# Block attention that feeds two dense layers: the attention step taken for two pairs of heads at a time

## Chip, cores and metric

The kernel runs on one core of a Trainium2 chip. The metric is the device time of one execution in microseconds (us); lower is better.

## What is computed

q, k and v have shape (2, 8, 768, 64): 2 batches, 8 heads, 768 tokens, 64 channels. A query sees its neighbours closer than 16 tokens and, beside them, one summary column for each of the 24 blocks of 32 tokens: the maximum of the block's keys and the mean of its values. The result, 1536 tokens by 512 channels, goes through two pairs of dense layers.

```python
k_sum = k.reshape(B, H, nb, block, D).max(axis=3)
v_sum = v.reshape(B, H, nb, block, D).mean(axis=3)
scores = concat([where(|i - j| < 16, q k^T / 8, -1e9), q k_sum^T / 8 + log(32)])
a = exp(scores - max);  a = a / (sum(a) + 1e-9)
x = (a @ concat([v, v_sum])).transpose(0, 2, 1, 3).reshape(1536, 512)
h = x @ moe_w_in;   x = (h * clip(h + 3, 0, 6) / 6) @ moe_w_out      # w_in 512x2048, w_out 2048x512
h = x @ moe2_w_in;  out = (h * cos(h)) @ moe2_w_out
```

The dense weights arrive with 8 bytes an element, read by the kernel as pairs of 32-bit words.

## The kernel before

**Attention.** The 8 heads make 4 pairs; a pair fills 128 partitions (two heads of 64 channels). The work is cut into 24 units `(b, h, p)`: batch, third of the sequence (256 tokens), pair. One unit is one call of `att`:

- `score`: 8 products, each 64 channels by 64 queries against 120 columns (96 tokens around the queries and 24 summaries). In 32-bit floats each product is two matmul instructions, so 16. They use TensorE in tiles of 64x64 and write two banks of PSUM (`c_s`), one for each head of the pair.
- four times VectorE adds the mask and takes the maximum (L529), and ScalarE takes the exponential and its sum (L537).
- GpSimd, VectorE and either of them: sum plus 1e-9, its reciprocal, the multiplication (L546, L551, L555).
- `trans`: four transposes on the whole array into the one bank of `c_t` (L564), and a copy to `pt`.
- `pv`: 8 products (16 instructions) with tiles of 128 rows by 64 columns (L573), into the one bank of `c_o`; then `xh`, a copy rounded to the type `F32R`, and `xl`, what the rounding left (256 columns each).

For each batch and pair, `load_k` and `load_v` bring keys and values (576 KB each), `k_prep` takes the maxima (L497), and `vsum_pe` takes the block means with two TensorE products in tiles of 32 columns (L477: 24 instructions; L482: 2), two small copies and `fill`, which writes the means into all 12 windows of `vw`. `load_q` brings 128 KB for each unit into one of three buffers `z`.

**Dense layers.** Every product is made as three passes, high by high, high by low and low by high part (L667 to L669 for the first product of a layer pair, L743 for the second). A chunk of 128 of the 2048 inner columns has two halves of weights, each split into its parts by ScalarE, VectorE and GpSimd (L618, L622, L627, then L403 or L405, and L410). Blocks are 512 tokens, except that the very first block is two of 256 tokens. A first product needs `x` of all four pairs for its tokens. `post` makes the nonlinearity and the two parts of `g`.

**Order.** `Plan` holds every operation with its cost in us on the engines that may do it, a priority, and the buffers it takes. `order()` runs a list schedule over these costs on the host, and the instructions are issued in the order that it finds; each engine and the SP queue, which issues nearly all transfers, then work in that fixed order. `refine()` repeats this five times with priorities that come from deadlines. The numbers in `T` set the first priorities: `A0` and `AS` when unit after unit starts, `lk`, `lq`, `lv` the loads, `kp`, `vpe`, `fill` the preparation, `g0`, `gi`, `wc`, `wl` the dense layers; `nz`, `nraw`, `n2` and the like are counts of buffers. Up to `busy` us, small idle matmuls (L434, on the identity) fill gaps of TensorE in the plan. The cost of a TensorE operation is a constant, whatever stood ahead of it (`score` 0.58, `trans` 0.44, `pv` 0.62).

Buffers that only attention uses are given back when its last operation is issued (`turn`), and more buffers for the dense layers (`w`, `g`, `n`, `r`) take their place.

Of the kernel before, what the change touches and what calls it, by code (L numbers as in the profile page):

```python
# [18 lines left out]
P = 128  # L19
# [43 lines left out]
def consts():  # L63
# [53 lines left out]
class Op:  # L117
    __slots__ = ("engs", "fn", "prio", "port", "seq", "wait", "after", "ready", "takes", "uses", "start", "eng", "took")


class Plan:
# [10 lines left out]
    def op(self, engs, fn, prio, r=(), w=(), take=(), port=0.0):  # L132
        o = Op()
        o.engs, o.fn, o.prio, o.port, o.seq = engs, fn, prio, port, len(self.ops)
# [87 lines left out]

    def refine(self):
        best = None
        for n in range(T["n"]):
            if n:
                self.reset()
            try:
                order = self.order()
            except AssertionError:  # L230
                break
            end, late = self.deadlines(order)
            if best is None or end < best[0] - 1e-9:
                best = (end, [o.prio for o in self.ops])
            for o in self.ops:
                if "PE" not in o.engs:
                    o.prio = late[id(o)]
        self.end = best[0]
        for o, p in zip(self.ops, best[1]):
            o.prio = p  # L240
        self.reset()

    def order(self):
# [6 lines left out]
        free["DMA"] = T["d0"]  # L250

# [11 lines left out]
        while events:  # L263
# [11 lines left out]
            for e in names:  # L275
# [79 lines left out]
def body(ctx: ExitStack, tc: tile.TileContext, q, k, v, w_in1, w_out1, w_in2, w_out2, ident_d, mask_d, avg_d, out):  # L355
# [34 lines left out]
    c_r = slots("r", 2, [P, TOK], later=T["n2"])  # L390
# [62 lines left out]
    def load_q(b, h, p, prio):  # L453
        z = Buf(c_z)
        dma(lambda: z.t, lambda: q[b, p][:, HT * P * h:HT * P * h + HT * P], 0.54, prio, w=[z], take=[z])
        return z
# [13 lines left out]
    def vsum_pe(vw, prio):  # L470
# [3 lines left out]
        def mm(e):  # L474
            for s in range(NS):
                a, g = 2 * (NS - 1 - s), s % 4 * QD
                nc.tensor.matmul(out=bank.t[g:g + QD, 0:P], lhsT=avg[0:CW, a:a + QD], rhs=vw.t[0:CW, s, :],  # L477
                                 start=(s < 4), stop=(s >= NS - 4), tile_position=(0, g))
# [3 lines left out]
        op({"PE": 0.25}, lambda e: nc.tensor.matmul(out=bank.t[CW:P, P:2 * P], lhsT=avg[:, AW:AW + QD], rhs=y.t,  # L482
                                                    start=True, stop=True, tile_position=(0, CW)),
           prio, r=["avg", y], w=[bank])
        op({"ACT": 0.2, "DVE": 0.2}, lambda e: copy(e, x.t[CW:CE, :], bank.t[CW:CE, P:2 * P]), prio, r=[bank],
           w=[(x, 0), (x, 1)])
        return x

    def fill(x, vw, prio):
        op({"POOL": 1.5, "ACT": 1.55},  # L490
           lambda e: copy(e, vw.t[CW:CE, :, :], x.t[CW:CE, :].rearrange("p (u f) -> p u f", u=1).to_broadcast([NB, NS, P])),
           prio, r=[(x, 0), (x, 1)], w=[(vw, CW)], take=[vw])
# [12 lines left out]
    def att(b, h, p, kw, z, vw, prio, banks):  # L505
        sp = [Buf(banks) for _ in range(2)]
        e_, sm, pt, tp, res = Buf(c_e), Buf(c_sm), Buf(c_pt), Buf(c_t), Buf(c_o)
        N4 = 2 * HT
        subs = [(i, u, o) for i in range(HT) for u in range(2) for o in range(2)]

        def score(e):
            for i, u, o in subs:
                f = slice(D * o, D * o + D)
                a = i * P + u * SUB
                nc.tensor.matmul(  # L515
                    out=sp[o].t[u * SUB:u * SUB + SUB, i * CE:i * CE + CE], lhsT=z.t[f, a:a + SUB],
                    rhs=kw.t[f, 2 * (HT * h + i) + u, :], start=True, stop=True,
                )

        op({"PE": 0.58}, score, prio,  # L520
           r=[z, (kw, "own"), (kw, "sum")], w=sp, take=[*sp, e_, sm])
        for i in range(HT):
            t = HT * h + i
            mk = mask[:, 0 if t == 0 else (2 if t == TB - 1 else 1), :]
            for o in range(2):
                x = 2 * i + o
                op(
                    {"DVE": 0.2},
                    lambda e, i=i, o=o, x=x, mk=mk: nc.vector.tensor_tensor_reduce(  # L529
                        out=e_.t[:, x, :], in0=sp[o].t[:, i * CE:i * CE + CE], in1=mk,  # L530
                        scale=-0.125, scalar=3.0e38, op0=ALU.add, op1=ALU.min, accum_out=sm.t[:, x:x + 1],
                    ),
                    prio, r=[sp[o], "masks"], w=[(e_, x), (sm, x)],
                )
                op(
                    {"ACT": 0.38},
                    lambda e, x=x: nc.scalar.activation(  # L537
                        out=e_.t[:, x, :], in_=e_.t[:, x, :], func=ACTF.Exp, scale=-1.0,
                        bias=sm.t[:, x:x + 1], accum_out=sm.t[:, N4 + x:N4 + x + 1],
                    ),  # L540
                    prio, r=[(sm, x)], w=[(e_, x), (sm, N4 + x)],
                )
        sums = [(sm, N4 + x) for x in range(N4)]
        op(
            {"POOL": 0.2},
            lambda e: nc.gpsimd.tensor_scalar(  # L546
                out=sm.t[:, N4:2 * N4], in0=sm.t[:, N4:2 * N4], scalar1=1.0, scalar2=1e-9, op0=ALU.mult, op1=ALU.add
            ),
            prio, w=sums,
        )  # L550
        op({"DVE": 0.09}, lambda e: nc.vector.reciprocal(out=sm.t[:, N4:2 * N4], in_=sm.t[:, N4:2 * N4]), prio,  # L551
           w=sums)
        op(
            {"POOL": 1.05, "DVE": 0.57},
            lambda e: eng[e].tensor_tensor(  # L555
                out=e_.t, in0=e_.t,
                in1=sm.t[:, N4:2 * N4].rearrange("p (x u) -> p x u", u=1).to_broadcast([P, N4, CE]), op=ALU.mult,
            ),
            prio, r=sums, w=[(e_, x) for x in range(N4)], port=0.5,
        )  # L560

        def trans(e):
            for x in range(N4):
                nc.tensor.transpose(out=tp.t[0:CE, x * P:(x + 1) * P], in_=e_.t[:, x, :], identity=ident)  # L564

        op({"PE": 0.44}, trans, prio, r=[(e_, x) for x in range(N4)], w=[tp], take=[tp, pt])
        op({"ACT": 0.49, "DVE": 0.6}, lambda e: copy(e, pt.t[0:CE, :], tp.t[0:CE, :]), prio, r=[tp], w=[pt])

        def pv(e):
            for i, u, o in subs:  # L570
                f = slice(D * o, D * o + D)
                a, c = (2 * i + o) * P + u * SUB, i * P + u * SUB
                nc.tensor.matmul(out=res.t[f, c:c + SUB], lhsT=vw.t[0:CE, 2 * (HT * h + i) + u, f],  # L573
                                 rhs=pt.t[0:CE, a:a + SUB], start=True, stop=True)
# [4 lines left out]
        hi, lo, r = xh[j][:, p, c], xl[j][:, p, c], range(i, i + HT)  # L579
        op({"ACT": 0.28, "DVE": 0.34}, lambda e: copy(e, hi, res.t[:, 0:HT * P]), prio, r=[res],  # L580
           w=[("xh", j, p, i) for i in r])
        op({"DVE": 0.33}, lambda e: sub(e, lo, res.t[:, 0:HT * P], hi), prio,
           r=[res, *(("xh", j, p, i) for i in r)], w=[("xl", j, p, i) for i in r])
# [4 lines left out]
    units = []  # L588
# [3 lines left out]
    for y, (b, h, p) in enumerate(units):  # L592
        pr = A0 + AS * HT * y
        if h == 0:
            kws[p], ks = load_k(b, p, pr + T["lk"])
        z = load_q(b, h, p, pr + T["lq"])
        if h == 0:
            vws[p] = load_v(b, p, pr + T["lv"])
# [225 lines left out]
```

## Time and profile before

| what | us |
|---|---|
| median of 3 runs | 610.3 (610.02 to 610.71) |
| the profiled execution, its own time | 610.45 |
| its span, first to last instruction | 608.7 |
| TensorE busy in the span | 602.1 (99%) |
| VectorE, GpSimd, ScalarE busy | 387.2, 347.0, 268.8 |

The span is 1.75 us shorter than the execution's own time. The granted TensorE clock is 1.00 of full speed (2.4 GHz) in every stretch of 10 us. A matmul's busy time in these views is longer than the step from its start to the next one's start, because matmuls overlap; where a time on TensorE is worked out below, it is taken from starts.

### The profile page before, as it was taken

How to read it: one execution, taken by the hardware profiler on the slowest of the kernel's cores; microseconds unless marked ns; L12 is line 12 of the kernel's file. 1: busy time of each engine (PE TensorE's matmuls, PEld its weight loads, DVE VectorE, ACT ScalarE, POOL GpSimd, SP SyncE). 2: the span in 40 equal slices, each digit the busy share in tenths (PEclk: the TensorE clock that was granted, in tenths of full speed). 3: DMA queues.
4: the chain of work that ended last, by engine and by line, in shares of the span. 5: the costliest groups of instructions: out<-in, count | busy, mean ns of one | idle time of the engine just before them, and what ended most of it. 6: DMA issues, size and time to landing. Idle time of an engine off the chain costs nothing.

```text
span 608.7 us, 9662 instructions
## 1 busy us (share of the span) xinstructions
PE 602.1 (99%) x3636; PEld 498.6 (82%) x3636; DVE 387.2 (64%) x724; ACT 268.8 (44%) x585; POOL 347.0 (57%) x366
## 2 busy tenths in 40 slices
PE   9999999999999999999999999999999999999997
PEld 8878877788888888888888888888888888888886
DVE  3599894443852258523993589857984897574562
ACT  2698886533421114301351547654752363343240
POOL 2588784555853438623688398656864577443340
PEclk9999999999999999999999999999999999999999
DMA  9978950042420004300440013301320020000112
GB/s 224 269 240 246 255 184 22 1 138 70 138 70 0 1 7 167 105 0 1 140 137 0 1 69 104 104 2 68 105 103 2 1 103 1 1 2 0 70 42 97
DMA packets 28334, 50.07 MB, mean 82 GB/s; under 512 B 14464, under 2 KB 17920, under 8 KB 28288
## 3 DMA queue, kind: packets, MB, share of 16 engines
q1 hardware_dynamic: 28144, 49.40, 26.4%
q8 instruction: 28, 0.46, 0.3%
q14 instruction: 18, 0.15, 0.1%
q10 hardware_dynamic: 144, 0.07, 0.0%
HBM read 46.31 MB, written 3.15 MB: 81 GB/s over the span
## 4 chain that ended last, share of the span: by engine, by line
PE 94%; DVE 2%; POOL 1%; ACT 1%; issue 1%; DVEq 0%; POOLq 0%; ACTq 0%
PE acc L743 25%; PE s L743 18%; PE h L667 8%; PE h L668 8%; PE h L669 8%; PE o L669 3%; PE t L669 3%; PE o L667 3%; PE t L667 3%; PE o L668 3%; PE t L668 3%; PE acc L434 2%; PE s L515 2%; PE o L573 2%; PE t L564 2%; PE h L477 1%
## 5 line engine op out<-in xcount | busy, mean ns | idle before, releaser
L405 POOL TENSOR_SCALAR g<-r 128x512 fp32r<-128x512 f32 (+1 forms) x81 | 61.9, 764 | 135.4 <-DVE r L718 40.8
L410 POOL TENSOR_TENSOR g<-r,g 128x512 fp32r<-128x512 f32 (+1 forms) x73 | 100.5, 1377 | 7.3 <-ACT g L403 2.8
L699 ACT ACTIVATE n<-h,bias 128x512 f32<-128x512 f32 (+1 forms) x60 | 39.3, 656 | 141.3 <-PE h L669 139.3
L743 PE MATMUL acc<-g,w 128*128 128x512 f32 (+1 forms) x432 | 96.0, 370 | 0.0
L667 PE MATMUL h<-xh,w 128*128 128x512 f32 (+1 forms) x240 | 92.5, 386 | 0.0
L668 PE MATMUL h<-xl,w 128*128 128x512 f32 (+1 forms) x240 | 90.0, 375 | 0.0
L669 PE MATMUL h<-xh,w 128*128 128x512 f32 (+1 forms) x240 | 90.0, 375 | 0.0
L743 PEld LDWEIGHTS acc<-g,w 128*128 128x128 f32 x432 | 75.3, 188 | 14.3 <-issue 0.8
L703 DVE SCALAR_TENSOR_TENSOR r<-n,h 128x512 f32<-128x512 f32 (+1 forms) x60 | 38.7, 646 | 56.8 <-ACT n L699 31.0
L743 PE MATMUL acc<-w,g 128*128 128x512 f32 x288 | 69.2, 389 | 0.0
L743 PE MATMUL s<-w,g 128*128 128x512 f32 x288 | 69.2, 389 | 0.0
L410 POOL TENSOR_TENSOR w<-cf,w 128x512 fp32r<-128x512 f32 x44 | 64.1, 1460 | 3.3 <-ACT w L403 1.6
L743 PEld LDWEIGHTS acc<-w,g 128*128 128x128 f32 x288 | 54.1, 188 | 11.2
L743 PEld LDWEIGHTS s<-w,g 128*128 128x128 f32 x288 | 54.0, 188 | 11.2
L627 DVE SCALAR_TENSOR_TENSOR cf<-cu,cf 128x512 uint32<-128x512 uint32 x64 | 60.0, 955 | 0.4
L618 ACT ACTIVATE cu<-raw 128x512 f32<-128x512 f32 x64 | 42.9, 670 | 38.5 <-DVE cf L627 23.7
L622 DVE TENSOR_SCALAR cf<-raw 128x512 uint32<-128x512 uint32 x64 | 47.3, 755 | 11.8 <-POOL w L410 11.6
L667 PEld LDWEIGHTS h<-xh,w 128*128 128x128 f32 x240 | 45.1, 188 | 9.9 <-issue 1.7
L711 POOL TENSOR_SCALAR n<-n 128x512 f32<-128x512 f32 x45 | 31.8, 707 | 37.3 <-ACT n L699 37.2
L669 PEld LDWEIGHTS h<-xh,w 128*128 128x128 f32 x240 | 45.1, 188 | 8.2
L668 PEld LDWEIGHTS h<-xl,w 128*128 128x128 f32 x240 | 45.1, 188 | 7.8
L405 POOL TENSOR_SCALAR w<-cf 128x512 fp32r<-128x512 f32 x41 | 31.4, 770 | 30.3 <-DVE cf L627 23.2
(95 smaller groups left out, 1054.7 us busy)
## 6 DMA issues: line engine op xcount, KB each, us to landing
raw<-in_w_in_dram SPq DMA_DIRECT2D x32, 512.0 KB, 4.1
raw<-in_w_out_dram SPq DMA_DIRECT2D x32, 512.0 KB, 3.7
kw<-in_k_dram SPq DMA_DIRECT2D x8, 576.0 KB, 6.0
vw<-in_v_dram SPq DMA_DIRECT2D x8, 576.0 KB, 9.3
z<-in_q_dram SPq DMA_DIRECT2D x24, 128.0 KB, 5.7
out_dram<-part SPq DMA_DIRECT2D x8, 256.0 KB, 2.0
out_dram<-kw SPq DMA_DIRECT2D x3, 256.0 KB, 2.0
out_dram<-kw SPq DMA_DIRECT2D x2, 128.0 KB, 1.7
```

The lines of the kernel that those rows point to most:

```text
L405: eng[e].tensor_scalar(out=out, in0=in_, scalar1=scale, scalar2=0.0, op0=ALU.mult, op1=ALU.add)
L410: eng[e].tensor_tensor(out=out, in0=in0, in1=in1.bitcast(F32), op=ALU.subtract)
L618: lambda e, raw=raw, u=u: nc.scalar.activation(out=u.t, in_=raw.t.bitcast(F32)[:, :, 1], func=ACTF.Prelu, scale=2.0 ** -112, alpha=2.0 ** 32),
L622: lambda e, raw=raw, f=f: eng[e].tensor_scalar(out=f.t.bitcast(U32), in0=raw.t[:, :, 0], scalar1=2.0 ** -29, scalar2=7.0, op0=ALU.mult, op ...
L627: lambda e, u=u, f=f: nc.vector.scalar_tensor_tensor(out=f.t.bitcast(U32), in0=u.t.bitcast(U32), scalar=3, in1=f.t.bitcast(U32), op0=ALU.l ...
L667: nc.tensor.matmul(out=o, lhsT=wh, rhs=hi, start=(kk == 0), stop=False)
L668: nc.tensor.matmul(out=o, lhsT=wh, rhs=lo, start=False, stop=False)
L669: nc.tensor.matmul(out=o, lhsT=wl, rhs=hi, start=False, stop=(kk == KT - 1))
L699: op({"ACT": t(fixed, 0.43)}, lambda e: nc.scalar.activation(out=out(), in_=in_(), func=func, **kw), pr, r=rd, w=wr, take=take)
L703: op({"DVE": t(0.09, 0.56)}, lambda e: nc.vector.scalar_tensor_tensor(out=out(), in0=a(), scalar=s, in1=b(), op0=o0, op1=o1), pr, r=rd, w= ...
L711: op({"POOL": t(0.16, 0.47), "DVE": t(0.07, 0.265)}, lambda e: eng[e].tensor_scalar(out=n(), in0=n(), scalar1=1.0, scalar2=-MAGIC, op0=ALU ...
L743: nc.tensor.matmul(out=o, lhsT=l, rhs=r, start=(c == 0 and z == 0), stop=(c == GS - 1 and z == 2))
```

## The change

Attention is taken for two pairs of heads at a time. The units become `(b, h, p, ny)`: the first two stay single, and then there are 11 of two pairs each. In such a unit `score` issues 16 products in one go (columns 0 to 479 of the same two banks), and `pv` 16 into one whole bank of `c_o`; `xh` and `xl` are made once for 512 columns. The mask, exponential, sums, multiplication, transposes and copies to `pt` stay as they were, pair by pair. `load_q` moves both pairs at once (256 KB). `vsum_pe` takes the values of two pairs: 48 instructions into one bank, one copy, one second product over 256 columns, one copy; `fill` stays one for each pair.

Buffers: `z` 3 of one pair become 2 of two, `vs` 2 become 1 of two, `e` 3 become 2 of two, `sm` 4 become 2 of two; `r` of the dense layers has 1 in place of 2 until `turn`.

The plan: every TensorE operation has a tiling `mode` (0 dense, 1 transpose, 2 score, 3 pv, 4 sums of v), and `change(a, b)` adds a price where it differs from the one before. The costs of the attention operations are set without it. All numbers in `T` are new.

```diff
 T = dict(
-    A0=6.982, AS=1.584, mask=-12.92, kp=-20.41, qp=-33.47, lk=-17.33, lq=-11.81, lv=-4.43, vs=33.64, vss=-16.92,
-    vsp=-29.27, wl=-1.64, wc=-25.07, g0=20.77, gi=7.33, pp=27.42, fill=-9.73, DVE=1.348, POOL=0.497, cold=5, d0=0.9,
-    warm=9, tail=1, lagq=1, nraw=3, ncf=2, n=5, w2=2, n2=3, g2=3, nz=3, busy=42, slack=0.2, vpe=-7.47, avg=-27.4,
+    A0=5.118, AS=1.568, mask=-8.22, kp=-14.19, qp=-15.92, lk=-15.36, lq=-11.42, lv=-4.09, vs=37.77, vss=27.87,
+    vsp=-18.03, wl=-15.78, wc=-15.19, g0=20.42, gi=5.51, pp=17.22, fill=-28.29, DVE=1.348, POOL=0.572, cold=5, d0=0.9,
+    warm=9, tail=1, lagq=3, nraw=3, ncf=2, n=5, w2=2, n2=3, g2=3, nz=2, nr=1, busy=42, slack=0.2, vpe=-45.26,
+    avg=-8.5,
 )
...
+    @staticmethod
+    def change(a, b):
+        if a == b:
+            return 0.0
+        return (0.165 if a > 1 else 0.0) + (0.19 if b > 1 else 0.1 if b else 0.0)
...
+                if e == "PE":
+                    cost += self.change(mode, o.mode)
+                    mode = o.mode
...
-    c_z = slots("z", T["nz"], [P, HT * P], pool=ap)
+    c_z = slots("z", T["nz"], [P, 2, HT * P], pool=ap)
...
-    c_vs = slots("vs", 2, [P, P], pool=ap)
-    c_y = slots("y", 1, [P, P], pool=ap)
+    c_vs = slots("vs", 1, [P, 2, P], pool=ap)
+    c_y = slots("y", 1, [P, 2, P], pool=ap)
...
-    c_e = slots("e", 3, [P, 2 * HT, CE], pool=ap)
-    c_sm = slots("sm", 4, [P, 4 * HT])
+    c_e = slots("e", 2, [P, 4 * HT, CE], pool=ap)
+    c_sm = slots("sm", 2, [P, 8 * HT])
...
-    c_r = slots("r", 2, [P, TOK], later=T["n2"])
+    c_r = slots("r", T["nr"], [P, TOK], later=T["n2"])
...
-        op({"PE": 0.85}, mm, prio, r=["avg", (vw, 0)], w=[bank], take=[bank, x, y])
-        op({"ACT": 0.2, "DVE": 0.2}, lambda e: copy(e, y.t, bank.t[:, 0:P]), prio, r=[bank], w=[y])
+            for i, vw in enumerate(vws):
...
+        op({"PE": 1.36}, mm, prio, r=["avg", *((vw, 0) for vw in vws)], w=[bank], take=[bank, x, y], mode=4)
+        op({"ACT": 0.3, "DVE": 0.34}, lambda e: copy(e, both(y.t), bank.t[:, 0:2 * P]), prio, r=[bank], w=[y])
...
+            for y in range(ny):
+                for i, u, o in subs:
...
-        op({"PE": 0.58}, score, prio,
+        op({"PE": 0.41 * ny}, score, prio,
+           r=[z, *((kw, x) for kw in kws for x in ("own", "sum"))], w=sp, take=[*sp, e_, sm], mode=2)
...
-        op({"PE": 0.44}, trans, prio, r=[(e_, x) for x in range(N4)], w=[tp], take=[tp, pt])
+            op({"PE": 0.425}, trans, prio, r=[(e_, x) for x in xs], w=[tps[y]], take=[tps[y], pts[y]], mode=1)
...
-        op({"PE": 0.62}, pv, prio, r=[pt, (vw, 0), (vw, CW)], w=[res], take=[res])
+        op({"PE": 0.44 * ny}, pv, prio, r=[*pts, *((vw, x) for vw in vws for x in (0, CW))], w=[res], take=[res], mode=3)
...
-    for p in range(NP + T["lagq"]):
-        units += [(0, 0, p)] * (p < NP) + [(0, 1, p - T["lagq"])] * (p >= T["lagq"])
-    units += [(b, h, p) for b in range(B) for h in range(NH) for p in range(NP) if b or h > 1]
+    units = [(0, 0, 0, 1), (0, 0, 1, 1), (0, 0, 2, 2)]
+    units += [(b, h, p, 2) for b in range(B) for h in range(NH) for p in range(0, NP, 2) if b or h]
```

## Rows read from the trace of the kernel before

**Rows 1.** Page, part 4: the chain that ended last, share by engine.
```profile
PE 94%; DVE 2%; POOL 1%; ACT 1%; issue 1%; DVEq 0%; POOLq 0%; ACTq 0%
```
**Rows 2.** Busy time by stretch: start and end, length, us (instructions) of each engine, clock, DMA.
```profile
0.00:26.00 26.00, 24.94 (x282) 22.83 (x282) 9.86 (x51) 10.10 (x39) 8.46 (x20) 1.00 1.00 250
26.00:53.00 27.00, 25.23 (x381) 20.96 (x379) 25.61 (x91) 24.05 (x81) 21.38 (x24) 1.00 0.78 243
53.00:90.00 37.00, 36.80 (x537) 30.48 (x535) 34.54 (x121) 32.46 (x116) 29.53 (x35) 1.00 0.81 217
90.00:118.00 28.00, 28.00 (x299) 21.33 (x297) 12.17 (x61) 18.09 (x63) 13.75 (x19) 1.00 0.09 30
118.00:605.18 487.18, 487.14 (x2150) 403.03 (x2148) 304.25 (x402) 184.04 (x291) 273.92 (x269) 1.00 0.17 57
```
**Rows 3.** Chain that ended last, stretches 26 to 54 us, then 53 to 118, by line.
```profile
by line: DVE cf L627 15.9%; issue 10.0%; DVE cf L622 8.3%; POOL w L405 8.0%; DVE w L410 6.3%; PE s L515 6.2%; ACT e L537 5.8%; DVE e L529 5.7%; POOL e L555 5.0%; POOL w L410 4.6%; DVE xl L410 3.9%; PE t L564 3.5%; PE h L477 2.8%; PE o L573 
...
by line: PE acc L743 22.9%; PE o L573 13.3%; PE t L564 11.4%; PE h L667 11.1%; PE s L515 10.5%; PE h L668 8.1%; PE h L669 8.0%; PE h L477 3.7%; POOL e L555 2.2%; POOL w L410 2.0%; ACT e L537 1.8%; PE h L482 1.0%; ACT pt L403 0.9%; ACT cu L6
```
**Rows 4.** Timeline of PE around one score; last two from windows inside it (start, us).
```profile
102.28 0.39 PE L669 MATMUL h<-xh,w 128*128 128x512 f32 x1
102.60 0.64 PE L515 MATMUL s<-kw,z 64*64 64x120 f32 x16
103.17 0.50 PE L667 MATMUL h<-xh,w 128*128 128x512 f32 x1
103.51 0.40 PE L668 MATMUL h<-xl,w 128*128 128x512 f32 x1
...
102.86 0.39 PE L515 MATMUL s<-kw,z 64*64 64x120 f32 x8
102.96 0.28 PE L515 MATMUL s<-kw,z 64*64 64x120 f32 x4
```
**Rows 5.** The same around one pv.
```profile
106.34 0.39 PE L669 MATMUL h<-xh,w 128*128 128x512 f32 x1
106.66 0.69 PE L573 MATMUL o<-pt,vw 120*64 120x64 f32 x16
107.27 0.50 PE L667 MATMUL h<-xh,w 128*128 128x512 f32 x1
107.61 0.40 PE L668 MATMUL h<-xl,w 128*128 128x512 f32 x1
...
106.94 0.40 PE L573 MATMUL o<-pt,vw 120*64 120x64 f32 x8
107.06 0.29 PE L573 MATMUL o<-pt,vw 120*64 120x64 f32 x4
```
**Rows 6.** Stretch 53 to 118 us, lines L515, L573, L477: PE (instructions), PEld, clock, DMA.
```profile
53.00:118.00 65.00, 8.34 (x208) 5.36 (x208) 1.00 0.50 137
53.00:118.00 65.00, 10.94 (x256) 8.79 (x256) 1.00 0.50 137
53.00:118.00 65.00, 3.45 (x96) 2.38 (x96) 1.00 0.50 137
```
**Rows 7.** Groups of instructions: evacuation of one pair, and copies of 512 columns.
```profile
L403 ACT ACTIVATE xh<-o 128x256 fp32r<-128x256 f32 x23 | 8.7, 378 | 3.5 <-PE o L573 3.4
L410 DVE TENSOR_TENSOR xl<-o,xh 128x256 fp32r<-128x256 f32 x24 | 10.0, 417 | 12.0 <-ACT xh L403 11.8
L403 ACT ACTIVATE part<-acc 128x512 f32<-128x512 f32 x8 | 4.7, 591 | 3.1 <-PE acc L743 3.1
L766 DVE TENSOR_TENSOR part<-part,acc 128x512 f32<-128x512 f32 x26 | 17.7, 682 | 19.3 <-PE acc L743 19.3
```
**Rows 8.** Timelines of PE and of the SP queue in the first 37 us.
```profile
19.03 4.90 PE L434 MATMUL acc<-ident 128*128 128x64 f32 x42
23.86 0.86 PE L477 MATMUL h<-vw,avg 96*32 96x128 f32 x24
35.14 0.39 PE L667 MATMUL h<-xh,w 128*128 128x256 f32 x1
36.21 0.86 PE L477 MATMUL h<-vw,avg 96*32 96x128 f32 x24
...
18.80 0.33 SPq L437 DMA_DIRECT2D raw<-in_w_in_dram  x1
26.91 0.33 SPq L437 DMA_DIRECT2D z<-in_q_dram  x1
27.29 0.44 SPq L437 DMA_DIRECT2D vw<-in_v_dram  x1
```

More of the change, by code (lines that the diff above doesn't have):

```diff
@@ L117 @@
 class Op:
-    __slots__ = ("engs", "fn", "prio", "port", "seq", "wait", "after", "ready", "takes", "uses", "start", "eng", "took")
+    __slots__ = ("engs", "fn", "prio", "port", "seq", "wait", "after", "ready", "takes", "uses", "start", "eng", "took", "mode")
 class Plan:
@@ L483, in vsum_pe, with fill @@
                                                     start=True, stop=True, tile_position=(0, CW)),
-           prio, r=["avg", y], w=[bank])
-        op({"ACT": 0.2, "DVE": 0.2}, lambda e: copy(e, x.t[CW:CE, :], bank.t[CW:CE, P:2 * P]), prio, r=[bank],
-           w=[(x, 0), (x, 1)])
+           prio, r=["avg", y], w=[bank], mode=4)
+        op({"ACT": 0.3, "DVE": 0.34}, lambda e: copy(e, both(x.t)[CW:CE, :], bank.t[CW:CE, 2 * P:4 * P]), prio, r=[bank],
+           w=[x])
         return x
-    def fill(x, vw, prio):
+    def fill(x, i, vw, prio):
@@ L509, in att @@
         subs = [(i, u, o) for i in range(HT) for u in range(2) for o in range(2)]
         def score(e):
[L512 to L518, printed above, removed]
-        op({"PE": 0.58}, score, prio,
-           r=[z, (kw, "own"), (kw, "sum")], w=sp, take=[*sp, e_, sm])
@@ L543, in att @@
[L543 to L560, printed above, removed]
@@ new lines, in att @@
+        op({"PE": 0.41 * ny}, score, prio,
+           r=[z, *((kw, x) for kw in kws for x in ("own", "sum"))], w=sp, take=[*sp, e_, sm], mode=2)
+        for x in range(N8):
+            i, o = divmod(x, 2)
+            t = HT * h + i % HT
+            mk = mask[:, 0 if t == 0 else (2 if t == TB - 1 else 1), :]
+            op(
+                {"DVE": 0.2},
+                lambda e, i=i, o=o, x=x, mk=mk: nc.vector.tensor_tensor_reduce(
+                    out=e_.t[:, x, :], in0=sp[o].t[:, i * CE:i * CE + CE], in1=mk,
+                    scale=-0.125, scalar=3.0e38, op0=ALU.add, op1=ALU.min, accum_out=sm.t[:, x:x + 1],
+                ),
+                prio, r=[sp[o], "masks"], w=[(e_, x), (sm, x)],
+            )
+            op(
+                {"ACT": 0.38},
+                lambda e, x=x: nc.scalar.activation(
+                    out=e_.t[:, x, :], in_=e_.t[:, x, :], func=ACTF.Exp, scale=-1.0,
+                    bias=sm.t[:, x:x + 1], accum_out=sm.t[:, N8 + x:N8 + x + 1],
+                ),
+                prio, r=[(sm, x)], w=[(e_, x), (sm, N8 + x)],
+            )
@@ new lines, in att, with trans @@
+        for y in range(ny):
+            xs = range(y * N4, y * N4 + N4)
+            sums = [(sm, N8 + x) for x in xs]
+            a = slice(N8 + y * N4, N8 + y * N4 + N4)
+            op(
+                {"POOL": 0.2},
+                lambda e, a=a: nc.gpsimd.tensor_scalar(
+                    out=sm.t[:, a], in0=sm.t[:, a], scalar1=1.0, scalar2=1e-9, op0=ALU.mult, op1=ALU.add
+                ),
+                prio, w=sums,
+            )
+            op({"DVE": 0.09}, lambda e, a=a: nc.vector.reciprocal(out=sm.t[:, a], in_=sm.t[:, a]), prio, w=sums)
+            op(
+                {"POOL": 1.05, "DVE": 0.57},
+                lambda e, y=y, a=a: eng[e].tensor_tensor(
+                    out=e_.t[:, y * N4:y * N4 + N4, :], in0=e_.t[:, y * N4:y * N4 + N4, :],
+                    in1=sm.t[:, a].rearrange("p (x u) -> p x u", u=1).to_broadcast([P, N4, CE]), op=ALU.mult,
+                ),
+                prio, r=sums, w=[(e_, x) for x in xs], port=0.5,
+            )
+            def trans(e, y=y, xs=xs):
+                for x in xs:
+                    c = (x - y * N4) * P
+                    nc.tensor.transpose(out=tps[y].t[0:CE, c:c + P], in_=e_.t[:, x, :], identity=ident)
+            op({"PE": 0.425}, trans, prio, r=[(e_, x) for x in xs], w=[tps[y]], take=[tps[y], pts[y]], mode=1)
+            op({"ACT": 0.49, "DVE": 0.6}, lambda e, y=y: copy(e, pts[y].t[0:CE, :], tps[y].t[0:CE, :]), prio, r=[tps[y]],
+               w=[pts[y]])
@@ new lines, in pv @@
+        def pv(e):
+            for y in range(ny):
+                for i, u, o in subs:
+                    f = slice(D * o, D * o + D)
+                    a, c = (2 * i + o) * P + u * SUB, (y * HT + i) * P + u * SUB
+                    nc.tensor.matmul(out=res.t[f, c:c + SUB], lhsT=vws[y].t[0:CE, 2 * (HT * h + i) + u, f],
+                                     rhs=pts[y].t[0:CE, a:a + SUB], start=True, stop=True)
+        op({"PE": 0.44 * ny}, pv, prio, r=[*pts, *((vw, x) for vw in vws for x in (0, CW))], w=[res], take=[res], mode=3)
@@ L577, in att @@
         j, i = divmod(b * TB + HT * h, QT)
         c = slice(i * P, (i + HT) * P)
[L579 to L583, printed above, removed]
+        hi, lo = xh[j][:, p:p + ny, c], xl[j][:, p:p + ny, c]
@@ L585, in body, with both @@
+        his, los = ([(x, j, p + y, t) for y in range(ny) for t in range(i, i + HT)] for x in ("xh", "xl"))
+        def both():
+            return res.t[:, 0:ny * HT * P].rearrange("p (y c) -> p y c", y=ny)
+        op({"ACT": 0.07 + 0.21 * ny, "DVE": 0.07 + 0.27 * ny}, lambda e: copy(e, hi, both()), prio, r=[res], w=his)
+        op({"DVE": 0.06 + 0.27 * ny}, lambda e: sub(e, lo, both(), hi), prio, r=[res, *his], w=los)
     A0, AS = T["A0"], T["AS"]
@@ L587, in body @@
     kws, vws = {}, {}
-    units = []
-    for p in range(NP + T["lagq"]):
-        units += [(0, 0, p)] * (p < NP) + [(0, 1, p - T["lagq"])] * (p >= T["lagq"])
-    units += [(b, h, p) for b in range(B) for h in range(NH) for p in range(NP) if b or h > 1]
[L592 to L598, printed above, removed]
-            fill(vsum_pe(vws[p], pr + T["vpe"]), vws[p], pr + T["fill"])
-            k_prep(kws[p], ks, pr + T["kp"])
-        att(b, h, p, kws[p], z, vws[p], pr, c_s)
+    units = [(0, 0, 0, 1), (0, 0, 1, 1), (0, 0, 2, 2)]
+    units += [(b, h, p, 2) for b in range(B) for h in range(NH) for p in range(0, NP, 2) if b or h]
+    n = 0
+    for b, h, p, ny in units:
+        pr = A0 + AS * HT * n
+        n += ny
+        ps = range(p, p + ny)
+        both = (p, p + 1) if h == 0 and p % 2 == 0 else ()
+        for y in both:
+            kws[y], ks = load_k(b, y, pr + (y - p) * AS * HT * (ny < 2) + T["lk"])
+            k_prep(kws[y], ks, pr + T["kp"])
+        z = load_q(b, h, p, ny, pr + T["lq"])
+        for y in both:
+            vws[y] = load_v(b, y, pr + T["lv"])
+        if both:
+            x = vsum_pe([vws[y] for y in both], pr + T["vpe"])
+            for y in both:
+                fill(x, y - p, vws[y], pr + T["fill"])
+        att(b, h, p, [kws[y] for y in ps], z, [vws[y] for y in ps], pr)
     pl.first = len(pl.ops)
```

71 lines of the change are left out of this document (28 added, 43 removed).

## Prediction

> **What bounds the kernel now.** I read the shares of the chain that ended last, then the busy time by stretch, then the chain of single stretches, then TensorE's timeline around single attention operations. TensorE carries 94% of the chain [rows 1], so the question is what its time consists of. By stretch [rows 2] there are four parts. Up to 26 us the transfers set the pace: the 16 DMA engines are full (share 1.00) and VectorE works 9.86 us of 26. From 26 to 53 us VectorE is busy 25.61 of 27, and the chain runs through the weights' conversion and the softmax on VectorE and GpSimd [rows 3], not through TensorE; what TensorE saves there buys nothing by itself. From 53 to 118 us the chain is nearly all TensorE [rows 3]: attention operations between dense products, TensorE busy 64.80 of 65. From 118 us on there are dense products alone, 2150 in 487.18 us, so 0.227 us each, with no gap [rows 2]. That last part the change doesn't touch, apart from which engine does which copy or subtraction (the plan's factor for GpSimd goes from 0.497 to 0.572); TensorE's products cover that as long as VectorE, with 304.25 of 487.18 us, keeps its slack. So the time is that of the first 118 us: whatever makes the last attention operation end earlier, with the same amount of dense work done by then, comes off the end one for one.
>
> **Price of one visit to attention's tiling.** Around one score [rows 4] the last dense product before starts at 102.28 and the second one after at 103.51. Of these 1.23 us two dense steps are 0.45; the visit costs 0.78. It has an entry (102.28 to 102.60, less a step: 0.09) and an exit (103.17 to 103.51, less a step: 0.11), together 0.20. Inside, four instructions take 0.10 (102.86 to 102.96), so the 16 of a second pair add 0.40 to a visit that is already open. Two visits cost 1.56, one of twice the length 1.18: 0.38 saved. For pv [rows 5]: 1.27 less 0.45 is 0.82 for a visit, four instructions take 0.12, a second pair adds 0.48, and one double visit in place of two saves 0.34. For the block means no row shows a visit between two dense products. Each visit spared saves at least entry and exit of the score's, 0.20, and by the nearest row not more than its 0.38; I take 0.20, since the second product gets longer columns.
>
> **How many visits, in the stretch where they count.** Between 53 and 118 us there are 208/16 = 13 scores, 256/16 = 16 pv and 96/24 = 4 means, with 4 second products [rows 6]. Halved, this spares 6.5, 8, 2 and 2 visits: 6.5 x 0.38 + 8 x 0.34 + 4 x 0.20 = 2.5 + 2.7 + 0.8 = 6.0 us. Where a visit stands directly beside another attention operation there is no dense product to come back to, and no entry or exit to spare. I take a fourth of the 18.5 spared visits for such: 4.6 x 0.20 = 0.9 off. That leaves 5.1 us; the bounds are 18.5 x 0.20 = 3.7 less 0.9, and 18.5 x 0.38 = 7.0. Transposes keep their number and are no term.
>
> **Between 26 and 53 us.** What counts is VectorE. Mask, maximum, reciprocal and the copies of transposes stay. `xl` for 512 columns costs, by VectorE's subtraction-like addition of 512 columns out of PSUM, 0.682 in place of 2 x 0.417: 0.15 less for two pairs; on ScalarE `xh` goes from 2 x 0.378 to 0.591, 0.17 less [rows 7]. Seven units lie in this stretch, so 3.5 x 0.15 = 0.5 us of VectorE's chain. Half the small copies of the means go as well, on whichever of the two engines is free; I add nothing. Bounds 0 and 1.
>
> **The start.** Three things change. TensorE sat on idle matmuls for 4.90 us from 19.03, since the next instruction in its fixed order, the means of the second pair's values, waited for their transfer until 23.86 [rows 8]. Means now wait for both pairs' values in any case, so this wait stays. The SP queue stood still from 18.80 to 26.91: a load of q waited for one of three buffers, and behind it the last pair's values were issued only at 27.29 and used at 36.21 [rows 8]. With two buffers of two pairs (the two single units take one each) the third load, for pairs 2 and 3, waits for the first score alone; that helps. And the first dense product needs `x` of all four pairs for 256 tokens: the four units that make it now stand first in the list, where three units of the next third stood among them. Against this, pairs 2 and 3 now wait for each other. Bounds: 4.9 us gained, or the loss of the rival below; I take 0.4 us gained. The smaller counts of buffers cost nothing in the sum: `e` and `sm` still hold four pairs, and the single `r` is covered by TensorE's attention work; with that cover gone each dense nonlinearity would wait for the one before it.
>
> **Sum.** 5.1 + 0.5 + 0.4 = 6.0 us. The profiled execution took 610.45, 0.15 above the median; 604.45 by it, **604.3** against the median.
>
> **Rivals.**
> 1. *VectorE holds the pace.* From 53 to 90 us it is busy 34.54 of 37 [rows 2], and it must still do every mask, maximum and subtraction. If TensorE only waits more there, the 5.1 us count in the last 28 of the 65 us alone: 2.2, with the other terms 3.1, so 607.3. For it: 93% busy. Against it: from 90 to 118 us VectorE is busy 12.17 of 28 [rows 2], so the next 15.8 us are free, and weights not yet needed can move there. Beside it stands a rule of the Trainium skill, TensorEngine Tiling (Array Packing), section "PSUM Bottleneck": tiling speeds up TensorE but not the evacuation of PSUM, whose copies may become the bottleneck. By that rule this rival is what happens; the rows of 26 to 53 us agree with it, those of 90 to 118 do not.
> 2. *The start gains as well.* If the idle matmuls' 4.90 us [rows 8] or as much in 26 to 53 us becomes work, another 4.9: 599.4. For it: the first tokens need four units in place of seven. Against it: transfers are full up to 26 us, and no byte is saved.
> 3. *Slower: pairs 2 and 3 wait for each other at the start.* From the second pair's means (23.86) to the first dense product (35.14) took 11.3 us [rows 8]. If no dense product can run before the last values are in, and these come as late as before (36.21), the same way ends at 47.5, 12.4 us later. TensorE would have attention in a part of it; I price two thirds, 8 us: 612.3. It decides against the change from 6.0 us on. Against it: nothing holds that load back any more but the queue's order.
> 4. *Nothing comes of it.* With one bank for transposes the second pair's wait for the copy of the first, pv waits for both, and TensorE's spared time comes back as waits: 609.9.
>
> **Chances.** Forecast 0.50, rival 1 0.20, rival 2 0.14, rival 3 0.10, rival 4 0.06. The measurement tells 0.2%, 1.2 us, from no change. Faster by more: 0.50 + 0.14 + most of rival 1 (0.18) = 0.82; within: 0.06 + 0.02 = 0.08; slower: 0.10. The forecast's own range by its bounds is 602.4 to 606.5. To leave out no more than 2 in 10 the range takes in rivals 1 and 2: 598.6 to 609.0.
>
> **What would show it.** L515 and L573 stand in 13 visits each, 11 of them of 32 instructions; a double score between dense products spans 1.18 us beyond the dense steps, a double pv 1.30. The last pv ends near 112 us and dense products run from there as before, 487 us minus what was done ahead. If VectorE holds the pace, TensorE has waits on L529 or L410 between 53 and 84 us, and the chain leaves TensorE there. If rival 3 is right, the first dense product starts after 41 us. The prediction is wrong if the stretch after the last pv shows gaps, or if the same visits are spared and the idle time up to 53 us grows by as much.

## The result: 3.6 us slower

The changed kernel takes 614.07 us (613.81 to 614.34) where the kernel before takes 610.5 (610.02 to 610.97) beside it: 1.0058 of its time, 95% interval 1.0045 to 1.007. Forecast were 604.3 and a range of 598.6 to 609.0. A few executions, of the kernel before too, take 8 to 18 us more at no lower granted clock (628 against 610), and every median below leaves these out.

The stretches of [rows 2] in the changed kernel (busy us and instructions of PE, PEld, DVE, ACT, POOL; clock; DMA):

```profile
0.00:26.00 26.00, 24.94 (x246) 24.10 (x249) 9.15 (x49) 8.26 (x34) 4.87 (x16) 1.00 0.85 223
26.00:53.00 27.00, 25.81 (x412) 22.42 (x405) 22.31 (x67) 21.58 (x62) 19.13 (x21) 1.00 0.83 243
53.00:118.00 65.00, 62.11 (x828) 52.57 (x828) 46.68 (x180) 49.55 (x166) 45.20 (x59) 1.00 0.53 147
118.00:608.00 490.00, 489.99 (x2218) 405.34 (x2217) 308.72 (x417) 188.73 (x308) 279.00 (x270) 1.00 0.17 57
```

TensorE looks as full as before up to 53 us, but the other engines work less there: GpSimd 24.0 us in place of 29.8, VectorE 31.5 in place of 35.5, and the transfers fall from a share of 1.00 to 0.85 in the first 26 us. That points at TensorE as what holds the others back. From 53 to 118 us it has gaps of 2.9 us, where it had 0.2. The last pv starts at 126.1 us, where it started at 117.8.

What TensorE is busy with is seen in its groups. First the kernel before (columns: count, busy us, mean ns, idle before):

```profile
L434 PE MATMUL acc<-ident 128*128 128x64 f32 x146 | 18.2, 277 | 0.0
L573 PE MATMUL o<-pt,vw 120*64 120x64 f32 x384 | 16.5, 228 | 0.8 <-DVE xl L410 0.8
L515 PE MATMUL s<-kw,z 64*64 64x120 f32 x384 | 16.4, 275 | 0.8 <-DVE sm L529 0.7
L477 PE MATMUL h<-vw,avg 96*32 96x128 f32 x192 | 6.9, 277 | 0.0
L482 PE MATMUL h<-y,avg 128*32 128x128 f32 x16 | 3.2, 285 | 0.0
```

The same groups in the changed kernel (line 447 is the idle matmul, 600 pv, 538 score, 492 and 500 the means):

```profile
L447 PE MATMUL acc<-ident 128*128 128x64 f32 x212 | 26.0, 281 | 0.0
L600 PE MATMUL o<-pt,vw 120*64 120x64 f32 x384 | 14.1, 226 | 0.7 <-POOL vw L418 0.7
L538 PE MATMUL s<-kw,z 64*64 64x120 f32 x384 | 12.8, 270 | 0.0
L492 PE MATMUL h<-vw,avg 96*32 96x128 f32 x192 | 6.1, 275 | 0.0
L500 PE MATMUL h<-y,avg 128*32 128x256 f32 x8 | 2.5, 391 | 0.0
```

Attention's products fall from 43.0 to 35.5 us of busy time, 7.5 less. Idle matmuls rise from 18.2 to 26.0, 7.8 more. Busy times of neighbours overlap, so the balance is made from starts: each instruction counts up to the next one's start, less the gap before that one.

| TensorE, from starts (us) | before | changed | difference |
|---|---|---|---|
| idle matmuls | 17.31 | 25.30 | +7.99 |
| gaps (2.7 more from 53 to 118 us, 0.6 less up to there) | 1.97 | 4.08 | +2.11 |
| attention: score, pv, means, transposes | 49.38 | 43.55 | −5.83 |
| dense products (in 46 and 32 unbroken stretches) | 531.42 | 529.99 | −1.43 |
| behind the last matmul | 3.5 | 4.2 | +0.7 |

Together that is the 3.5 by which the span grows (612.2 against 608.7). So the spared visits are there, 7.3 us with the dense products beside them, and idle matmuls have taken their place: behind the first matmul and up to 53 us, idle matmuls and gaps take 26.5 us of TensorE in place of 19.1.

The place where they hurt first, on TensorE and on VectorE (start, us):

```profile
9.46 0.64 PE L538 MATMUL s<-kw,z 64*64 64x120 f32 x16
10.03 8.47 PE L447 MATMUL acc<-ident 128*128 128x64 f32 x74
18.34 0.61 PE L589 MATMUL t<-ident,e 128*120 128x128 f32 x4
18.87 0.64 PE L538 MATMUL s<-kw,z 64*64 64x120 f32 x16
...
12.74 0.77 DVE L579 TENSOR_TENSOR e<-e,sm 128x480 f32<-128x480 f32 x1
```

The transposes of the first unit start at 18.34, though VectorE had finished their input by 13.51. Between lie 74 idle instructions, 8.31 us or 0.112 each. One idle product is two instructions, so 0.225 us; the plan divides a gap by 0.11 to get their number. A planned gap is thus filled with about twice its length, and TensorE's order is fixed. Behind the second score (18.87) waits more: the SP queue stood until then with the next load of q, and the values of pairs 2 and 3 behind it, whose means came 13 us later:

```profile
19.60 0.39 SPq L450 DMA_DIRECT2D z<-in_q_dram  x1
21.02 0.90 SPq L450 DMA_DIRECT2D vw<-in_v_dram  x2
...
34.27 1.52 PE L492 MATMUL h<-vw,avg 96*32 96x128 f32 x48
```

### The profile page after: what moved, and what is told of

Same layout as the page of the kernel before. It is cut to its first block, busy times and chain, and to the rows that moved or that the text cites. A ratio compares the mean times of both kernels' runs of the same rounds, so it can differ in the third digit from the quotient of the medians.

```text
span 612.2 us, 9698 instructions
## 1 busy us (share of the span) xinstructions
PE 602.8 (98%) x3694; PEld 504.4 (82%) x3694; DVE 387.6 (63%) x713; ACT 268.1 (44%) x567; POOL 348.2 (57%) x365
## 4 chain that ended last, share of the span: by engine, by line
PE 92%; POOL 3%; DVE 3%; issue 1%; ACT 1%; DVEq 0%; ACTq 0%
PE acc L778 24%; PE s L778 18%; PE h L702 8%; PE h L703 8%; PE h L704 8%; PE acc L447 4%; PE o L703 3%; PE t L702 3%; PE o L702 3%; PE t L703 3%; PE t L704 3%; PE o L704 3%; PE t L589 1%; PE s L538 1%; PE o L600 1%
## 5 line engine op out<-in xcount | busy, mean ns | idle before, releaser
L423 POOL TENSOR_TENSOR g<-r,g 128x512 fp32r<-128x512 f32 (+1 forms) x83 | 111.6, 1345 | 8.7 <-ACT g L416 3.3
L423 POOL TENSOR_TENSOR w<-cf,w 128x512 fp32r<-128x512 f32 x46 | 67.5, 1471 | 3.6 <-ACT w L416 1.6
L418 POOL TENSOR_SCALAR w<-cf 128x512 fp32r<-128x512 f32 x44 | 33.4, 763 | 33.5 <-DVE cf L662 24.0
L746 POOL TENSOR_SCALAR n<-n 128x512 f32<-128x512 f32 x36 | 26.1, 725 | 38.9 <-ACT n L734 38.8
```

The source lines that it names most:

```text
L418: eng[e].tensor_scalar(out=out, in0=in_, scalar1=scale, scalar2=0.0, op0=ALU.mult, op1=ALU.add)
L423: eng[e].tensor_tensor(out=out, in0=in0, in1=in1.bitcast(F32), op=ALU.subtract)
L746: op({"POOL": t(0.16, 0.47), "DVE": t(0.07, 0.265)}, lambda e: eng[e].tensor_scalar(out=n(), in0=n(), scalar1=1.0, scalar2=-MAGIC, op0=ALU ...
```

## The experiments

Theory **filler**: the idle matmuls are twice as long as the gaps that they fill, and the change leaves more gaps. Rival **pairing**: pairs wait for each other's transfers, and the filler sits in a wait that would be there anyway. A third suspect is the **price** of tiling changes, which reorders everything. Each time stands beside the kernel before on the same chip, which gave 610.3 to 610.5 every time.

### e1, e2: filler of the right length

One line, in the changed kernel (e1) and in the kernel before (e2):

```diff
-                    for _ in range(int((o.start - last - T["slack"]) / (0.11 if last > T["cold"] else 0.22))):
+                    for _ in range(int((o.start - last - T["slack"]) / 0.227)):
```

> The changed kernel, with one number different: the plan divides a gap of TensorE by 0.227 us in place of 0.11 (0.22 in the first 5 us) to get its number of idle matmuls. Theory 'filler': each idle product is two instructions of 0.113 us, so a planned gap is filled with twice its time, the next operation in TensorE's fixed order starts late by what is too much (first transposes at 18.34 us although their input was ready by 13.6), and the changed plan has more gaps (212 idle instructions against 146, 7.8 us more). Then the time falls by 4 to 9 us, to 605 to 610, the first transposes start near 14 us and the first dense product near 31. Theory 'pairing': pairs wait for each other's transfers, and the filler only sits in a wait that is there anyway: within 1 us of 614.

> The kernel before, with the same one number different. Theory 'filler': it loses less, since it has fewer idle instructions: 120 by 26 us, 82 of them behind the first score, 9.3 us of which half is too much: 2 to 5 us faster, 605.5 to 608.5; the changed kernel with right filler is then faster than or level with this one by 0 to 3 us, since its TensorE spares some 5 us of visits. Theory 'pairing': within 1 us of 610.5, and the changed kernel stays 3 us or more behind it.

e1: 609.69 us, 0.9995 of the kernel before (0.9974 to 1.0016), 4.4 below the changed kernel. e2: 608.32, 0.998 (0.9947 to 1.0012), 2 down in the median, though the interval takes in no change: two of its nine runs took 613.8, the others 607.3 to 608.8. TensorE at the start of e1, then at 29.76 a wait:

```profile
9.72 4.01 PE L447 MATMUL acc<-ident 128*128 128x64 f32 x34
13.56 0.60 PE L589 MATMUL t<-ident,e 128*120 128x128 f32 x4
14.10 0.64 PE L538 MATMUL s<-kw,z 64*64 64x120 f32 x16
...
29.76 1.39 PE L492 MATMUL h<-vw,avg 96*32 96x128 f32 x24 [1.84 <-DMA vw<-in_v_dram]
```

The transposes come 4.8 us earlier, and the waits for the values, which the filler had hidden, show. In e2 the wait that the prediction read as one for a transfer until 23.86 [rows 8] is this:

```profile
16.19 2.44 PE L434 MATMUL acc<-ident 128*128 128x64 f32 x20
19.76 0.86 PE L477 MATMUL h<-vw,avg 96*32 96x128 f32 x24 [1.12 <-DMA vw<-in_v_dram]
```

In the kernel before, that transfer was issued at 11.29 and landed 9.7 us later, at 21.0. So of the idle matmuls from 19.03 to 23.86 the first 2.0 us covered a wait, and 2.8 us were filler alone.

The pairing rival's "within 1 us" falls for e1. But the filler theory had e1 level with e2 or up to 3 us below it, and it is 1.4 above in the median (608.2 to 613.0 against 607.3 to 613.8), so the filler isn't all. Counted as above, idle matmuls and gaps up to 53 us take 20.6 us in e1 and 15.2 in e2: with filler of the right length in both, TensorE has 5.4 us more without work in the changed kernel.

### e3: no filler at all

One number of T, `busy`, the time up to which gaps are filled:

```diff
-    busy=42
+    busy=0
```

> The changed kernel without any idle matmul after the first 18. Theory 'filler': the first transposes start near 14 us and so do all others, as with right filler, unless the granted clock falls in the gaps; at half clock the attention operations of the first 50 us, some 15 us at full clock, take up to twice as long, but mostly in waits: 604 to 612. Theory 'pairing': 612 to 616, and the first dense product stays at 36 us.

609.22 us, 0.998 of the kernel before (0.9964 to 0.9996), 4.9 below the changed kernel. The clock pays for it, and still it is worth it:

```profile
0.00:26.00 26.00, 14.65 (x192) 11.36 (x192) 11.35 (x56) 12.09 (x40) 8.94 (x21) 0.80 1.00 259
26.00:53.00 27.00, 22.63 (x319) 18.24 (x319) 22.18 (x84) 21.43 (x72) 18.43 (x22) 0.75 0.83 253
```

The granted clock is 0.80 and 0.75 of full speed up to 53 us (in a run of 610.36, one of the slower ones), where the filler held it at 1.00. Holding it with this filler cost more than it brought.

### e5, e6, e8, e9: the price of tiling changes

The price alone taken out of the changed kernel, with right filler (e5) and with the old filler (e6). The costs that were set without it stay, so the plan now counts a double score at 0.82 us.

```diff
                 if e == "PE":
-                    cost += self.change(mode, o.mode)
+                    pass
                     mode = o.mode
```

The price alone put into the kernel before, with right filler (e9) and with the old one (e8): `mode`, `change` and the costs 0.41, 0.425, 0.44, 0.68, 0.12 for a single unit.

> The changed kernel with right filler (0.227), and a change of tiling costs nothing in the plan. Beside e1 this takes out the price alone. If the price sends operations to worse places (it makes TensorE look 10 us busier, so other work is put off), this is faster than e1's 609.7 by 1 to 3 us. If the loss lies in the pairs themselves, it is within 1 us of e1, and TensorE has as much time without work by 118 us (27 us in e1, 20 in e2).

> The changed kernel with one part undone: a change of tiling costs nothing in the plan; pairs, buffers, T and the old filler (0.11) stay. With right filler this took 2.8 us off (609.7 to 606.9). Theory 'price and filler add up': the price is worth the same here, 614.1 less 2 to 4, so 610 to 612, and the filler is worth 3 to 5 (its share is taken in e5 at 606.9). Rival 'the price alone lost it': 608 or less, clearly below the kernel before even with the old filler.

> The kernel before with right filler and with the changed kernel's price of tiling changes and costs of single operations; units stay single, T stays. Price alone. If the price is what loses, slower than e2's 608.3 by 2 us or more; if the pairs lose, within 1 us of e2 or faster.

> The kernel before with the price of tiling changes and the costs that go with it, and with the old filler. With right filler the price made this kernel 14 us slower (622.4 against 608.3). If the price acts by the order of operations that it brings about, and not by the filler, 622 to 627 here as well. If it acted by the clock, which fell to 0.86 to 0.87 of full speed between 26 and 90 us with right filler, more filler holds the clock at 1.00 and the loss shrinks to 4 to 8 us: 614 to 618.

| us (median) | no price, old filler | no price, right filler | price, old filler | price, right filler |
|---|---|---|---|---|
| single units | 610.3 (before) | 608.32 (e2) | 623.72 (e8) | 622.35 (e9) |
| pairs | 617.17 (e6) | 606.67 (e5) | 614.07 (after) | 609.69 (e1) |

Against the kernel before, e5 is 0.9941 (0.9924 to 0.9957), e6 1.0108 (1.009 to 1.0126), e9 1.02 (1.0185 to 1.0216), e8 1.0214 (1.0175 to 1.0252). Price and filler were expected to add up; they don't. Without the price, pairs are 6.8 us slower than single units with the old filler and 1.7 faster with the right one (three runs of e5, 606.2 to 607.1): the filler turns the sign. With the old filler the price helps the pairs, by 3.1. The two kernels' idle matmuls, e6 and then e5:

```profile
L447 PE MATMUL acc<-ident 128*128 128x64 f32 x292 | 34.8, 276 | 0.0
...
L447 PE MATMUL acc<-ident 128*128 128x64 f32 x156 | 20.0, 281 | 0.0
```

e6 has 292 of them, 34.8 us; the changed kernel has 212. The plan with the price leaves less to fill, and here that outweighs what it loses otherwise. With single units the price loses 13 to 14 us under either filler. That loss isn't the clock's: from 26 to 90 us the clock is 0.87 and 0.86 in e9 and 1.00 and 0.95 in e8, and e8 is no faster.

### e16, e17: filler in between, with and without the price

0.17 in place of 0.227, as e1 (e16) and as e5 (e17).

> The changed kernel, filler at 0.17 a product in place of 0.11 or 0.227. If the price's order is worse in itself, the clock is 1.00 in every stretch and the time is 2 us or more above e17: 610 to 612. If e1 lost by the clock, the two are within 1 us of each other: 608 to 610.

> The same without the price. Its filler is a third longer than e5's (20.0 us there, 10 us saved against the old one): between e5's 606.9 and the old filler's 617.2, nearer to e5: 608 to 611.

610.35 us (0.9991 to 1.0011 of the kernel before) and 608.74 (0.996 to 0.9986). In e1 the clock was 0.94 between 26 and 53 us. Now it is 1.00 in both kernels, and the price still costs 1.6 us, between the two values expected (2 or more, and less than 1). From 53 to 90 us, e16 and then e17:

```profile
53.00:90.00 37.00, 34.66 (x495) 30.03 (x495) 30.41 (x101) 31.49 (x101) 29.72 (x38) 1.00 0.78 219
...
53.00:90.00 37.00, 36.72 (x534) 31.65 (x532) 32.52 (x115) 31.56 (x101) 29.91 (x39) 1.00 0.75 199
```

TensorE has gaps of 2.3 us with the price and 0.3 without, though VectorE does 2.1 us less work in the same time. So about half of the 3.0 us between e1 and e5 is the order that the price brings about. That the rest goes with e1's clock fits these numbers, but no run shows it by itself. The gaps go with the price in every kernel here: from 53 to 118 us they come to 1.1 to 6.6 us in all ten whose plan has it, and to 0.1 to 0.7 in all eight whose plan hasn't.

### e4, e7, e10: parts of the change by themselves

e4 makes all units single in the changed kernel (old filler); e7, with right filler, makes the means pair by pair; e10, with right filler, takes T of the kernel before.

```diff
-    units = [(0, 0, 0, 1), (0, 0, 1, 1), (0, 0, 2, 2)]
-    units += [(b, h, p, 2) for b in range(B) for h in range(NH) for p in range(0, NP, 2) if b or h]
+    units = []                                  # e4
+    for p in range(NP + 1):
+        units += [(0, 0, p, 1)] * (p < NP) + [(0, 1, p - 1, 1)] * (p >= 1)
+    units += [(b, h, p, 1) for b in range(B) for h in range(NH) for p in range(NP) if b or h > 1]
...
-            x = vsum_pe([vws[y] for y in both], pr + T["vpe"])
-            for y in both:
-                fill(x, y - p, vws[y], pr + T["fill"])
+        for y in both:                              # e7
+            x = vsum_pe([vws[y]], pr + T["vpe"])
+            fill(x, 0, vws[y], pr + T["fill"])
```

> The changed kernel, but every attention unit takes one pair of heads, in the order of the kernel before; means of v stay in twos, the plan keeps the price of tiling changes and the new numbers. If doubling spares TensorE its visits (forecast 5.2 us of score and pv between 53 and 118 us) and the loss is elsewhere, this is slower than the changed kernel, 616 to 621. If doubling itself brings the wait at the start, it is faster: 608 to 612.

> The changed kernel with right filler, and the means of v made pair by pair as before (two buffers of one pair for the result); scores and pv stay in twos. Theory 'pairs of v wait': in e1 TensorE stands in the means for the second pair's values, 1.2 us at 19.3 and 1.8 at 27.9, and the pv behind them is late; without it 1 to 3 us faster than e1, 606.5 to 608.7, less 0.8 us for the four visits that come back. Rival 'other engines set the pace': what is gained before 32 us comes back as waits between 40 and 90 us (2.5 + 2.2 us in e1); within 1 us of 609.7.

> The changed kernel with right filler and with T of the kernel before (two buffers z, one r). If the new numbers of T lose the time at the start, this is faster than e1's 609.7 by 1 us or more, to 606 to 608.5. If the pairs lose it, 609 to 614.

e4 takes 622.91 us (1.0184; 1.0129 to 1.024), slower as the visits want it, but above the 616 to 621 expected. The single units here have fewer buffers (each takes one of two double ones), a T that wasn't made for them and a clock of 0.91 from 53 to 90 us, so it doesn't weigh the doubling alone. e7: 614.9 (1.0086; 1.0057 to 1.0114), 5 us above e1: a miss for both theories. Its order has the clock at 0.87 and 0.95 from 26 to 90 us and gaps of 6.6 us from 53 to 118 us; why, isn't shown. e10: 611.94 (1.0029; 1.0017 to 1.0041), some 2 us above e1, with the clock at 0.93 up to 26 us where e1 has 1.00: against the old numbers of T, the new ones don't lose the time.

### e13: single units at the start alone

As e5, with the first 8 units single in the order of before and 8 double units after them.

> As e5 (pairs, no price, right filler), but the first 8 units, the tokens 0 to 511 of the first batch, are single and in the order of the kernel before; the other 16 stay in twos (8 double units). If pairing at the start keeps TensorE empty, 2 to 4 us of the 4 that are missing come back: 603 to 605, and TensorE has done more dense products by 53 us than in e5. If the start is set by the transfers whatever the units are, 606 to 609 (the visits of the first 8 units come back, mostly in empty time).

606.32 us (0.995; 0.9927 to 0.9973), 0.3 below e5. But its twelve runs go from 604.75 to 611.32, and with them the clock: the six at 0.999 or 1.000 over the span take 604.75 to 605.85, below e5's three at 1.000 (606.17 to 607.10). So at full clock pairing at the start costs about 1 us. More than that the transfers don't leave, it seems (share 1.00 up to 26 us).

### e12, e14, e15: numbers of T for each version

Numbers found by varying T and keeping what gave the plan an earlier end, equally long for pairs without price (e12), single units without price (e14) and pairs with price (e15), all with right filler. For e12:

```diff
+T = dict(A0=10.32, AS=1.471, mask=-3.87, kp=-35.14, qp=-10.89, lk=-16.46, lq=-13.94, lv=-2.2, vs=71.35, vss=43.31, vsp=28.4,
+         wl=-15.71, wc=-15.85, g0=18.38, gi=6.06, pp=48.77, fill=-7.11, DVE=1.663, POOL=0.511, cold=5, d0=0.9, warm=9, tail=1,
+         lagq=3, nraw=3, ncf=2, n=5, w2=2, n2=3, g2=3, nz=2, nr=1, busy=42, slack=0.2, vpe=-12.24, avg=8.06)
```

> As e5, with other numbers in T, looked for in the plan on the host with right filler. If T was what held the pairs back, 602 to 605; if not, 606 to 608. It is also the try at a version faster than both kernels.

> The kernel before with right filler, and numbers of T looked for in the same way and for as long. If T held back the single units as much as the pairs, 604 to 606 and the pairs' lead stays at some 1.5 us; if the old T suited the single units already, 607.5 to 608.5 and the pairs of e12 lead by 3 us or more.

> As e1 (pairs, price, right filler), with numbers of T looked for in the same way and for as long. If the price only unsettled a T that was found without it, this comes to e12's time within 1.5 us; if a plan that charges for changes of tiling, but doesn't choose by them, is the worse plan, it stays 3 us or more behind e12: 607 to 611.

e12: **602.59 us**, 0.9868 of the kernel before (0.9853 to 0.9883), faster than both kernels and 5.7 us below e2, the fastest with single units. e14: 612.4 (1.0027; 1.0007 to 1.0048), expected at 604 to 608.5: a miss. e15: 610.69 (1.0; 0.9991 to 1.0009). So of three searches one gained 4.1 us on the chip (e12 beside e5), and two lost 4.1 and 1.0 (e14 beside e2, e15 beside e1): an earlier end in the plan is no sure gain, and with one try for each version e12's lead may be in part luck. The stretches of e12:

```profile
0.00:26.00 26.00, 23.90 (x298) 21.77 (x299) 11.65 (x64) 12.56 (x41) 9.58 (x23) 1.00 0.99 262
26.00:53.00 27.00, 25.65 (x384) 22.41 (x383) 23.38 (x77) 24.42 (x83) 21.66 (x25) 1.00 0.90 260
53.00:118.00 65.00, 64.32 (x825) 54.21 (x825) 44.74 (x168) 50.87 (x160) 43.59 (x58) 1.00 0.43 125
```

The first dense product starts at 27.37 (35.14 before, [rows 8]), idle matmuls are down to 16.7 us, and the clock is full throughout. In the other two it isn't: 0.94 from 26 to 53 us in e14, 0.91 and 0.83 up to 53 us in e15. With less filler an order also has to leave no gap in which the clock falls, and the plan knows nothing of it. So the distance between e12 and these two is not that of pairs and price alone.

## Why the prediction was wrong

**The price of a visit: right.** A double score between dense products in the changed kernel:

```profile
99.62 0.39 PE L704 MATMUL h<-xh,w 128*128 128x512 f32 x1
99.94 1.05 PE L538 MATMUL s<-kw,z 64*64 64x120 f32 x32
100.92 0.50 PE L702 MATMUL h<-xh,w 128*128 128x512 f32 x1
101.26 0.40 PE L703 MATMUL h<-xl,w 128*128 128x512 f32 x1
```

1.64 us from 99.62 to 101.26, less two dense steps of 0.227: 1.19 (forecast 1.18). A double pv steps from 97.25 to the next product at 98.33, 1.08 against 0.61 in [rows 5]: 0.47 for the second pair (forecast 0.48). The copies came out at the forecast sizes too: 681 ns for `xl` and 591 for `xh` of 512 columns (0.682, 0.591), but four of the eleven `xh` ran on VectorE, at 688 ns, which takes back more than `xl` saved there. By starts, attention and the dense products beside it give 7.3 us in the whole kernel; forecast were 5.1 from 53 to 118 us.

**The step that failed: the start.** The prediction read TensorE's 4.90 us of idle matmuls as a wait for a transfer until 23.86 ("so this wait stays") and put the start at a gain of 0.4. Measured are 7.4 us more of idle matmuls and gaps up to 53 us (26.5 against 19.1). Idle matmuls are no sign of a wait: they are work in a fixed order, here twice as long as the gap that they were made for. The transfer had landed at 21.0, and in e2, with half of them, the same means start at 19.76 after a wait of 1.12 us. The changed plan has more gaps on TensorE in its first 42 us and puts in more filler (212 instructions against 146; 176 with single units, e4), each us of gap costs nearly a second one, and the SP queue, behind the scores, passes the delay on to the loads. Between the changed kernel and e1, which differ in this alone, lie 4.4 us; without the price, between e6 and e5, 10.5. The doubled filler could be read from [rows 8]: 42 instructions, so 21 products, from 19.03 to 23.86, 0.23 us each against the 0.11 in the code.

The sign that came true is one that the prediction names at its end and gives no chance: the same visits spared, and the idle time up to 53 us grown by as much. The last pv, forecast near 112 us, starts at 126.1.

**How far this reaches.** From 614.07 to the forecast of 604.3 it is 9.8 us. Right filler takes off 4.4 (e1), and no price 3.0 more (e5); 2.4 stay. The parts don't add: with the old filler, taking the price out loses 3.1. In e5 idle matmuls and gaps up to 53 us still take 21.0 us, 2.0 more than before, where the forecast had 0.4 less. And the old filler cost the kernel before about 2 us as well (e2), so about half of the 4.4 is no difference between the two kernels.

**53 to 118 us: half right.** The visits are spared, but gaps of 2.7 us more came up, behind GpSimd and, once, ScalarE:

```profile
PE t L589 <- POOL e L579: 0.8, 2, 0.5
PE o L600 <- POOL vw L418: 0.7, 1, 0.7
PE t L589 <- ACT n L734: 0.6, 1, 0.6
PE acc L778 <- POOL g L423: 0.6, 1, 0.6
```

(engine, line, releaser: us, times, longest). Rival 1 said that VectorE holds the pace here; none of these waits ends with VectorE. The rule beside it, of the Trainium skill's TensorEngine Tiling (Array Packing), section "PSUM Bottleneck", is that evacuation may become the bottleneck. e17 and e12 speak against both: the same evacuations, in pairs, and TensorE full to 36.72 of 37 us in one and 64.32 of 65 in the other. The gaps belong to the priced order. Nor do the smaller counts of buffers make them, as the prediction said: e12 has the same counts.

**26 to 53 us: overtaken.** VectorE is no longer full there (22.31 of 27), so 0.5 us less of it could not count.

**Rival 3** had the sign and not the mechanism: the first dense product came at 36.33, 1.2 later than before and not 12.4, and pairing at the start costs about 1 us (e13 beside e5, at full clock). A chance of 0.10 for all that is slower was too low, since the way in which time was lost is none of its cases: what the plan fills in is itself on the path. A slip without weight: ahead of the fourth pair's first unit the list of the kernel before has two units of the next third, not three.

**Open.** Why an order made with the price is worse (1.6 us in pairs at full clock, 13 to 14 with single units and the old T) isn't settled. `change` is charged after an operation is picked and takes no part in the choice, so it can't bring like operations together; that this is the reason was only argued. How much of e14's and e15's distance to e12 is the clock also stays open, as does which part of the change leaves TensorE with less to do up to 53 us in e1 and e5.

## What to carry to other kernels

Filler between operations of an in-order engine is work: compare its planned length with its step in the trace before reading it as a wait. When a list schedule is rebuilt, sum busy time by kind (useful, filler) and gaps; a saving in one column may stand in another. A change of grain and the schedule's own numbers should be tried together: the change as it was made gave +3.6 us, pairs with other numbers of T, right filler and no price −7.9. The plan's own end doesn't tell: two of three searches for T that moved it forward made the kernel slower.

## What the runs showed of the hardware

- A 32-bit idle product of 128x128 by 64 columns is two instructions of 0.112 us each at full clock (74 in 8.31 us, no gap between them), so a product that is there only to fill takes 0.225 us of TensorE's order.
- Without filler the granted clock was 0.80 and 0.75 in the first two stretches, and the kernel was still 4.9 us faster than with it.
- The granted clock differs between executions of one kernel, and the time goes with it: six of e13's twelve runs, at 0.999 or 1.000 over the span, took 604.75 to 605.85 us, the other six, at 0.991 to 0.997, 606.79 to 611.32. In e12, at 0.999 or 1.000 in all four, they took 602.2 to 602.7.
